# Depthwise-separable convolution: where the last third of the weights is scaled, and how the program ends

## Chip, cores and metric

The kernel runs on one core of a Trainium2 chip. The metric is the device time of one execution in microseconds (us). A run's "span" is the profiled execution, which is some 1.7 to 1.8 us shorter than the time taken for the same run.

Engine names in the profile: PE is TensorE, PEld its weight loads, DVE VectorE, ACT ScalarE, POOL GpSimd, SP the engine that issues the transfers. L162 is line 162 of the kernel concerned.

## The reference

With a depthwise kernel of 1x1 the reference comes down to this, in bf16, with x of 1x384x384x384 and pw of 384x384:

```python
out = x * dw[0, 0]                       # per channel
return einsum('bhwc,cd->bhwd', out, pw)  # 147456 rows x 384 x 384
```

## The kernel before

The channel factors dw are multiplied into pw once, so that x goes straight into the matmuls. The 147456 rows are worked in 288 "supertiles" of 512 rows. For each, VectorE transposes x in blocks of 32x32, and TensorE runs 48 matmuls on quarters of its array (32 rows of contraction each, four side by side; the 48 take 1.951 us). The four quarters hold partitions 0 to 31, 32 to 63 and so on ("quadrants"), and each reads its own copy of the scaled weights `w_r`: 6 blocks of 2 x 384 columns on all 128 partitions. ScalarE copies the results out of PSUM.

The weights are made at the start. pw comes in one transfer; a selection matrix, scaled with dw, spreads its rows to all quadrants by matmul; the results are copied to `w_r`:

```python
nc.sync.dma_start(pw_n[:], pw.rearrange("(k p) d -> p k d", p=P)).then_inc(s_pw, 16)
# (cut: then all loads of x and stores, in order of need)
w_eng = [1, 0, 1, 1, 1, 1]              # who copies block b: 1 ScalarE, 0 VectorE
# (cut)
nc.tensor.wait_ge(s_pw, 16)
for b in range(NB):                     # NB = 6
    # (cut: waits)
    for r in range(2):
        mm = nc.tensor.matmul(w_ps(b)[:, r, :],
            lhsT=sel_w[:, b // 2, 2 * (b % 2) + r, :], rhs=pw_n[:, b // 2, :], start=True, stop=True)
    mm.then_inc(s_w)
for b in (0, 2, 3):
    nc.tensor.wait_ge(*w_done[b])
```

The loop of TensorE leaves out the last four supertiles. Three of those are written out one by one, and the last is worked in two parts of 256 and 128 columns, so that its first part can be copied while the second is computed:

```python
with nc.tensor.Fori(0, NS // 2 - 2, 1) as it:        # NS = 288, two supertiles a round
    rv = nc.tensor.to_reg(it + 1)
    for s in range(2):
        supertile(s, rv)
supertile(0, NS // 2 - 1)
supertile(1, NS // 2 - 1)
supertile(0, NS // 2)
for ps, c0, c1 in ((1, 0, DS), (0, DS, D)):          # DS = 256: the split of the last
    # (cut: 48 matmuls of c1 - c0 columns)
```

Only the last store writes rows of 4 x 384 elements that lie together (3072 bytes); those before it write 768 bytes for each supertile that they hold.

## Time and profile before

| | before |
|---|---|
| time, median of the first 3 runs | 577.61 us (577.1 to 577.85) |
| profiled span | 575.3 us |
| TensorE busy | 567.2 us, 99% of the span |
| VectorE, ScalarE busy | 509.9 and 418.2 us |
| loop of matmuls starts | 7.67 us |
| last copy out of PSUM ends | 569.98 us, 562.31 after the loop's start |
| last store issued, landed | 570.1, 574.0 us |

The middle is bound by TensorE (1.951 us a supertile). So the table is to be read from its lower half: what comes ahead of the loop, and what follows the last matmul, is all that the change can move. The lines that carry this are in the prediction.

### The profile page before, as it was taken

How to read it: one execution, taken by the hardware profiler on the slowest of the kernel's cores; microseconds unless marked ns; L12 is line 12 of the kernel's file. 1: busy time of each engine (PE TensorE's matmuls, PEld its weight loads, DVE VectorE, ACT ScalarE, POOL GpSimd, SP SyncE). 2: the span in 40 equal slices, each digit the busy share in tenths (PEclk: the TensorE clock that was granted, in tenths of full speed). 3: DMA queues.
4: the chain of work that ended last, by engine and by line, in shares of the span. 5: the costliest groups of instructions: out<-in, count | busy, mean ns of one | idle time of the engine just before them, and what ended most of it. 6: DMA issues, size and time to landing. Idle time of an engine off the chain costs nothing.

```text
span 575.3 us, 29802 instructions
## 1 busy us (share of the span) xinstructions
PE 567.2 (99%) x13919; PEld 415.8 (72%) x13919; DVE 509.9 (89%) x584; ACT 418.2 (73%) x297; POOL 1.7 (0%) x8
## 2 busy tenths in 40 slices
PE   8999999999999999999999999999999999999995
PEld 5777777777777777777777777777777777777774
DVE  6999999999999999999999999999999999999994
ACT  6777777777777777777777777777777777777774
POOL 1000000000000000000000000000000000000000
PEclk9999999999999999999999999999999999999999
DMA  8999999999999999999999999999999999998876
GB/s 344 429 399 428 425 415 428 428 430 409 376 411 419 374 399 430 397 390 389 432 398 389 397 429 388 389 401 432 387 394 410 423 390 391 409 402 320 369 282 227
DMA packets 25938, 226.92 MB, mean 394 GB/s; under 512 B 1221, under 2 KB 5702, under 8 KB 22086
## 3 DMA queue, kind: packets, MB, share of 16 engines
q1 hardware_dynamic: 25924, 226.79, 98.0%
q8 instruction: 3, 0.05, 0.0%
q14 instruction: 9, 0.07, 0.0%
q10 hardware_dynamic: 2, 0.00, 0.0%
HBM read 113.54 MB, written 113.25 MB: 394 GB/s over the span
## 4 chain that ended last, share of the span: by engine, by line
PE 98%; ACT 0%; DVE 0%; issue 0%; POOL 0%; POOLq 0%; SPq 0%
PE ps L162 97%; PE ps L181 0%; ACT w_r L292 0%; PE ps L241 0%; DVE O L322 0%; PE ps L212 0%; POOL zero L253 0%; POOL warm L252 0%; POOLq L355 0%; PE ps L196 0%; SPq L99 0%
## 5 line engine op out<-in xcount | busy, mean ns | idle before, releaser
L162 PE MATMUL ps<-w_r,T 32*128 32x384 bf16 x13776 | 559.8, 321 | 0.9 <-ACT w_r L292 0.9
L279 DVE STREAM_TRANSPOSE T<-X 128x384 uint32<-128x384 uint32 x576 | 505.9, 879 | 54.4
L325 ACT CAST O<-ps 128x1536 bf16<-128x1536 f32 x289 | 413.0, 1429 | 148.3 <-PE ps L162 147.7
L162 PEld LDWEIGHTS ps<-w_r,T 32*128 32x128 bf16 x13776 | 411.6, 93 | 149.1 <-issue 1.2
L292 ACT CAST w_r<-ps 128x768 bf16<-128x768 f32 x5 | 3.6, 820 | 1.9 <-PE ps L212 1.9
L181 PE MATMUL ps<-zero 32*128 32x384 bf16 x32 | 2.8, 517 | 1.4 <-POOL zero L253 1.4
L322 DVE CAST O<-ps 128x768 bf16<-128x768 f32 (+2 forms) x3 | 2.1, 691 | 1.4 <-PE ps L162 1.1
L297 DVE COPY dw_f<-ps 128x3 f32<-128x3 f32 x1 | 0.2, 160 | 3.0 <-PE ps L196 3.0
L212 PE MATMUL ps<-pw_n,sel_w 128*128 128x384 bf16 x12 | 2.7, 357 | 0.0
L181 PEld LDWEIGHTS ps<-zero 32*128 32x128 bf16 x32 | 1.1, 118 | 2.0 <-issue 1.7
L212 PEld LDWEIGHTS ps<-pw_n,sel_w 128*128 128x128 bf16 x12 | 1.0, 105 | 1.9 <-issue 0.7
L265 ACT ACT_TABLE_LOAD x1 | 1.3, 1283 | 1.5 <-SPq L99 1.5
L241 PE MATMUL ps<-w_r,T 32*128 32x256 bf16 (+1 forms) x96 | 2.2, 241 | 0.0
L241 PEld LDWEIGHTS ps<-w_r,T 32*128 32x128 bf16 x96 | 2.0, 93 | 0.2
L292 DVE CAST w_r<-ps 128x768 bf16<-128x768 f32 x1 | 1.0, 956 | 1.2 <-PE ps L212 1.2
L301 DVE TENSOR_SCALAR sel_w<-sel,dw_f 128x512 bf16<-128x512 bf16 x3 | 0.9, 347 | 0.1
L255 POOL TENSOR_SCALAR_AFFINE_SELECT sel<-ones 128x512 bf16<-128x512 bf16 x1 | 0.7, 735 | 0.1
L196 PEld LDWEIGHTS ps<-ones,dw_row 1*128 1x128 bf16 x3 | 0.3, 127 | 0.3 <-issue 0.2
L254 POOL MEMSET ones<- 128x512 bf16 x1 | 0.5, 528 | 0.0
L265 ACT COPY warm<-warm 128x1 f32<-128x1 f32 x2 | 0.3, 189 | 0.0
L253 POOL MEMSET zero<- 128x192 uint32 x1 | 0.3, 258 | 0.0
L196 PE MATMUL ps<-ones,dw_row 1*128 1x1 bf16 x3 | 0.3, 174 | 0.0
(5 smaller groups left out, 0.5 us busy)
## 6 DMA issues: line engine op xcount, KB each, us to landing
X<-in_x_dram SPq DMA_DIRECT2D x26, 3840.0 KB, 21.8
out_dram<-O SPq DMA_DIRECT2D x26, 3840.0 KB, 27.8
X<-in_x_dram SPq DMA_DIRECT2D x2, 1536.0 KB, 17.5
out_dram<-O SPq DMA_DIRECT2D x2, 1536.0 KB, 14.6
X<-in_x_dram SPq DMA_DIRECT2D x3, 768.0 KB, 7.5
out_dram<-O SPq DMA_DIRECT2D x3, 768.0 KB, 9.6
X<-in_x_dram SPq DMA_DIRECT2D x1, 2304.0 KB, 19.9
out_dram<-O SPq DMA_DIRECT2D x1, 2304.0 KB, 12.8
```

Of the source, the lines that this page charges most:

```text
L162: mm = nc.tensor.matmul(PS[s][:, q, :D], lhsT=Ts[s][32 * q : 32 * q + 32, b, par::2], rhs=w_r[32 * q : 32 * q + 32, b, par, :], start=(b = ...
L181: nc.tensor.matmul(PS[0][:, i % 4, :D], lhsT=zero[32 * (i % 4) : 32 * (i % 4) + 32, 0:P], rhs=zero[32 * (i % 4) : 32 * (i % 4) + 32, :], s ...
L196: mm = nc.tensor.matmul(PS[1][:, k, D : D + 1], lhsT=dw_row[:, P * k : P * k + P], rhs=ones[0:1, 0, 0:1], start=True, stop=True,)
L212: mm = nc.tensor.matmul(w_ps(b)[:, r, :], lhsT=sel_w[:, b // 2, 2 * (b % 2) + r, :], rhs=pw_n[:, b // 2, :], start=True, stop=True,)
L241: mm = nc.tensor.matmul(PS[ps][:, q, : c1 - c0], lhsT=Ts[1][32 * q : 32 * q + 32, b, par::2], rhs=w_r[32 * q : 32 * q + 32, b, par, c0:c1] ...
L255: nc.gpsimd.affine_select(out=sel[:].rearrange("p (v r) (q w) -> p v r q w", v=2, q=4), in_=ones[:].rearrange("p (v r) (q w) -> p v r q w" ...
L265: c = nc.scalar.copy(warm[:, s + 1 : s + 2], warm[:, 0:1])
L279: ins = nc.vector.transpose(out=Tw[:, 3 * h : 3 * h + 3], in_=Xw[:, :, j, 96 * h : 96 * h + 96].rearrange("p k (b w) -> p b k w", w=32),)
L292: i = nc.vector.tensor_copy(out, in_) if e == 0 else nc.scalar.copy(out, in_)
L301: nc.vector.tensor_scalar_mul(sel_w[:, k], sel[:], dw_f[:, k : k + 1]).then_inc(s_sw)
L322: e = nc.vector.tensor_copy(Ov[:, nq:4, j, c0:c1], PS[ps][:, nq:4, : c1 - c0])
L325: a = nc.scalar.copy(Ov[:, 0:nq, j, c0:c1], PS[ps][:, 0:nq, : c1 - c0])
```

## The change

Its intent: let the loop start earlier by making fewer weights ahead of it, and make the end shorter. It does four things.

1. Only two thirds of pw go through TensorE. The last third is loaded to each quadrant by a transfer of its own (four of 96 KB, 32 partitions each, issued after the first load of x), and GpSimd multiplies it by dw with four instructions of 128x384.
2. The loop waits at its entry for blocks 0 and 1 only. Blocks 2 to 5 are waited for within the first supertile.
3. The loop covers all 288 supertiles: no written-out end, no split.
4. The last three stores (and loads) use the layout with 3072-byte runs of output.

The diff, cut to its core:

```diff
-    pw_n = consts.tile([P, 3, D], BF16, name="pw_n")
+    pw_n = consts.tile([P, 2, D], BF16, name="pw_n")
+    pw_q = consts.tile([P, 2, 2, D], BF16, name="pw_q")
...
-            if t + 1 < NT:
-                dst = of[512 * first : 512 * (first + L), :].rearrange("(q p j) d -> p q (j d)", q=4, p=P)
+            if first + LONG < NS:                       # LONG = 3
+                dst = rows.rearrange("(q p j) d -> p q (j d)", q=4, p=P)
...
-        nc.sync.dma_start(pw_n[:], pw.rearrange("(k p) d -> p k d", p=P)).then_inc(s_pw, 16)
+        for k in range(2):
+            nc.sync.dma_start(pw_n[:, k, :], pw[P * k : P * k + P, :]).then_inc(s_pw[k], 16)
+        load_x(0)
+        pw_v = pw[2 * P :, :].rearrange("(b w r) d -> w b (r d)", w=32, r=2)
+        for q in range(4):
+            dst = pw_q[32 * q : 32 * q + 32].rearrange("w b r d -> w b (r d)")
+            nc.sync.dma_start(dst, pw_v).then_inc(s_pq, 16)
...
-        w_eng = [1, 0, 1, 1, 1, 1]
+        pieces = [(0, 0, 2, 1), (1, 0, 1, 0), (1, 1, 1, 1), (2, 0, 2, 1), (3, 0, 2, 1)]
+        pieces += [(b, r, 1, 2) for b in (4, 5) for r in range(2)]   # block, row, rows, engine (2: GpSimd)
...
+                        if s == 0 and par == 0 and q == 0 and b > 1:
+                            w_ready(b)
...
-        for b in (0, 2, 3):
-            nc.tensor.wait_ge(*w_done[b])
-        with nc.tensor.Fori(0, NS // 2 - 2, 1) as it:
+        for b in range(2):
+            w_ready(b)
+        with nc.tensor.Fori(0, NS // 2, 1) as it:
             rv = nc.tensor.to_reg(it + 1)
             for s in range(2):
                 supertile(s, rv)
-        supertile(0, NS // 2 - 1)
-        supertile(1, NS // 2 - 1)
-        supertile(0, NS // 2)
-        (the split last supertile)
...
+            if e == 2:
+                i = nc.gpsimd.tensor_scalar_mul(out, pw_q[:, b - 4, r : r + n, :], dw_q[:, ...])
+                i._wait_ge(s_pq, 64)
```

`dw_q`, dw laid out for the quadrants, comes from four small matmuls. The last supertile's results are now copied half by ScalarE and half by VectorE, in one go.

More of the change, by code (lines that the diff above doesn't have):

```diff
@@ L14 @@
 NR = 3
-DS = 256
+LONG = 3
 def _groups(n_super: int):
@@ L65 @@
     psum = ctx.enter_context(tc.tile_pool(name="psum", bufs=1, space=bass.MemoryType.PSUM))
-    pw_n = consts.tile([P, 3, D], BF16, name="pw_n")
+    pw_n = consts.tile([P, 2, D], BF16, name="pw_n")
+    pw_q = consts.tile([P, 2, 2, D], BF16, name="pw_q")
     ones = consts.tile([P, 4, P], BF16, name="ones")
     sel = consts.tile([P, 4, P], BF16, name="sel")
-    sel_w = consts.tile([P, 3, 4, P], BF16, name="sel_w")
+    sel_w = consts.tile([P, 2, 4, P], BF16, name="sel_w")
     w_r = consts.tile([P, NB, 2, D], BF16, name="w_r")
     dw_row = consts.tile([1, C], BF16, name="dw_row")
+    dw_b = consts.tile([P, 1], BF16, name="dw_b")
+    dw_q = consts.tile([P, 4], F32, name="dw_q")
     dw_f = consts.tile([P, 3], F32, name="dw_f")
@@ L88 @@
     s_dw = nc.alloc_semaphore("s_dw")
-    s_pw = nc.alloc_semaphore("s_pw")
+    s_pw = [nc.alloc_semaphore(f"s_pw{k}") for k in range(2)]
+    s_pq = nc.alloc_semaphore("s_pq")
     s_df = nc.alloc_semaphore("s_df")
@@ L92 @@
     s_dwf = nc.alloc_semaphore("s_dwf")
+    s_dq = nc.alloc_semaphore("s_dq")
+    s_dwq = nc.alloc_semaphore("s_dwq")
     s_sel = nc.alloc_semaphore("s_sel")
     s_w = nc.alloc_semaphore("s_w")
-    s_wr = [nc.alloc_semaphore(f"s_wr{e}") for e in range(2)]
+    s_wr = [nc.alloc_semaphore(f"s_wr{e}") for e in range(3)]
     s_seed = nc.alloc_semaphore("s_seed")
@@ L102, in load_x @@
             dst = Xs[g % NR][:, 4 * off : 4 * (off + L), :]
-            if t + 1 < NT:
-                src = xf[512 * first : 512 * (first + L), :].rearrange("(p s) c -> p (s c)", p=P)
+            rows = xf[512 * first : 512 * (first + L), :]
+            if first + LONG < NS:
+                src = rows.rearrange("(p s) c -> p (s c)", p=P)
                 dst = dst.rearrange("p s c -> p (s c)")
             else:
-                src = xf[512 * first :, :].rearrange("(a k q) c -> q a k c", k=4, q=4)
+                src = rows.rearrange("(a k q) c -> q a k c", k=4, q=4)
             if i == 0 and g >= NR:
@@ L116, in store @@
             src = Os[g % NR][:, 4 * off * D : 4 * (off + L) * D]
-            if t + 1 < NT:
-                dst = of[512 * first : 512 * (first + L), :].rearrange("(q p j) d -> p q (j d)", q=4, p=P)
+            rows = of[512 * first : 512 * (first + L), :]
+            if first + LONG < NS:
+                dst = rows.rearrange("(q p j) d -> p q (j d)", q=4, p=P)
                 src = src.rearrange("p (q e) -> p q e", q=4)
-                nc.sync.wait_ge(s_a[je % 2], je // 2 + 2)
-                if je >= NS - 2:
-                    nc.sync.wait_ge(s_d, 1)
-            else:
-                dst = of[512 * first :, :].rearrange("(m q) d -> m (q d)", q=4)
-                nc.sync.wait_ge(s_a[1], NS // 2 + 2)
-                nc.sync.wait_ge(s_d, 3)
+            else:
+                dst = rows.rearrange("(m q) d -> m (q d)", q=4)
+            nc.sync.wait_ge(s_a[je % 2], je // 2 + 2)
+            if je + 1 == NS:
+                nc.sync.wait_ge(s_d, 1)
             nc.sync.dma_start(dst, src).then_inc(s_o[g % NR], 16)
         nc.scalar.dma_start(dw_row[:], dw.rearrange("a e c -> a (e c)")).then_inc(s_dw, 16)
-        nc.sync.dma_start(pw_n[:], pw.rearrange("(k p) d -> p k d", p=P)).then_inc(s_pw, 16)
+        for k in range(2):
[5 more added lines that the diff above has]
+            nc.sync.dma_start(dst, pw_v).then_inc(s_pq, 16)
         todo = []
         for t, (g, i, off, first, L) in enumerate(chunks):
-            todo.append((g_end[g - NR] if g >= NR else -1, load_x, t))
+            if t > 0:
+                todo.append((g_end[g - NR] if g >= NR else -1, load_x, t))
             todo.append((first + L + 1, store, t))
@@ L140, with w_ready @@
             nc.sync.wait_ge(s_o[o], 16 * sum(map(len, groups[o::NR])))
-        w_eng = [1, 0, 1, 1, 1, 1]
-        w_done, made = [], [0, 0]
-        for e in w_eng:
+        pieces = [(0, 0, 2, 1), (1, 0, 1, 0), (1, 1, 1, 1), (2, 0, 2, 1), (3, 0, 2, 1)]
+        pieces += [(b, r, 1, 2) for b in (4, 5) for r in range(2)]
+        made = [0, 0, 0]
+        w_done = [[] for b in range(NB)]
+        for b, r, n, e in pieces:
             made[e] += 1
-            w_done.append((s_wr[e], made[e]))
+            w_done[b].append((s_wr[e], made[e]))
         def w_ps(b):
-            return PS[0 if b in (2, 3) else 1][:, 2 * (b % 2) : 2 * (b % 2) + 2, :D]
+            return PS[b // 2][:, 2 * (b % 2) : 2 * (b % 2) + 2, :D]
+        def w_ready(b):
+            for sem, v in w_done[b]:
+                nc.tensor.wait_ge(sem, v)
         def supertile(s, rv):
@@ L171, in supertile @@
                             mm._wait_ge(s_a[s], rv)
-                        elif s == 0 and q == 0 and par == 0:
-                            mm._wait_ge(*w_done[b])
                         if b in (2, 5) and par == 1 and q == 3:
@@ L196 @@
             mm = nc.tensor.matmul(
-                PS[1][:, k, D : D + 1],
+                PS[1][:, 0, D + k : D + k + 1],
                 lhsT=dw_row[:, P * k : P * k + P],
@@ L203 @@
         mm.then_inc(s_df)
-        idle_work(2)
-        nc.tensor.wait_ge(s_pw, 16)
-        for b in range(NB):
+        idle_work(1)
+        nc.tensor.wait_ge(s_sel, 1)
+        nc.tensor.wait_ge(s_dwf, 2)
+        for i in range(4):
+            mm = nc.tensor.matmul(
+                PS[1][:, 3, D + i : D + i + 1],
+                lhsT=sel[:, i, :],
+                rhs=dw_b[:],
+                start=True,
+                stop=True,
+            )
+        mm.then_inc(s_dq)
+        idle_work(1)
+        for b in range(4):
             if b % 2 == 0:
+                nc.tensor.wait_ge(s_pw[b // 2], 16)
                 nc.tensor.wait_ge(s_sw, b // 2 + 1)
-            if b >= 4:
-                nc.tensor.wait_ge(*w_done[b - 4])
+            if b == 2:
+                nc.tensor.wait_ge(s_dwq, 1)
             for r in range(2):
@@ L225 @@
                 supertile(s, rv)
-        supertile(0, NS // 2 - 1)
-        supertile(1, NS // 2 - 1)
-        supertile(0, NS // 2)
-        for ps, c0, c1 in ((1, 0, DS), (0, DS, D)):
-            for b in range(NB):
-                for par in range(2):
-                    for q in range(4):
-                        if par == 0 and q == 0:
-                            if ps == 1 and b in (0, 3):
-                                nc.tensor.wait_ge(s_t[1][b // 3], NS // 2)
-                            if b == 0:
-                                nc.tensor.wait_ge(s_a[ps], NS // 2 + (ps == 0))
-                                if ps == 0:
-                                    nc.tensor.wait_ge(s_d, 1)
-                        mm = nc.tensor.matmul(
-                            PS[ps][:, q, : c1 - c0],
-                            lhsT=Ts[1][32 * q : 32 * q + 32, b, par::2],
-                            rhs=w_r[32 * q : 32 * q + 32, b, par, c0:c1],
-                            start=(b == 0 and par == 0),
-                            stop=(b == NB - 1 and par == 1),
-                            tile_position=(32 * q, 0),
-                        )
-            mm.then_inc(s_pe)
         nc.gpsimd.memset(warm[:], 0.0).then_inc(s_seed)
@@ L287, with w_out @@
         order = [(t, j) for t in range(NT) for j in range(chunks[t][4])]
-        def w_out(b):
-            e = w_eng[b]
-            out, in_ = w_r[:, b, :, :], w_ps(b)
-            i = nc.vector.tensor_copy(out, in_) if e == 0 else nc.scalar.copy(out, in_)
-            i._wait_ge(s_w, b + 1)
+        def w_out(b, r, n, e):
+            out = w_r[:, b, r : r + n, :]
+            if e == 2:
+                i = nc.gpsimd.tensor_scalar_mul(out, pw_q[:, b - 4, r : r + n, :], dw_q[:, 2 * b + r - 8 : 2 * b + r - 7])
+                i._wait_ge(s_pq, 64)
+            else:
+                in_ = w_ps(b)[:, r : r + n, :]
+                i = nc.vector.tensor_copy(out, in_) if e == 0 else nc.scalar.copy(out, in_)
+                i._wait_ge(s_w, b + 1)
             i.then_inc(s_wr[e])
         nc.vector.wait_ge(s_df, 1)
-        nc.vector.tensor_copy(dw_f[:].rearrange("p (k o) -> p k o", o=1), PS[1][:, 0:3, D : D + 1]).then_inc(s_dwf)
+        nc.vector.tensor_copy(dw_f[:], PS[1][:, 0, D : D + 3]).then_inc(s_dwf)
+        nc.vector.tensor_copy(dw_b[:], PS[1][:, 0, D + 2 : D + 3]).then_inc(s_dwf)
         nc.vector.wait_ge(s_sel, 1)
         nc.vector.wait_ge(s_dwf, 1)
-        for k in range(3):
+        for k in range(2):
             nc.vector.tensor_scalar_mul(sel_w[:, k], sel[:], dw_f[:, k : k + 1]).then_inc(s_sw)
-        for b in range(NB):
-            w_out(b)
+        nc.vector.tensor_copy(dw_q[:], PS[1][:, 3, D : D + 4])._wait_ge(s_dq, 1).then_inc(s_dwq)
+        nc.gpsimd.wait_ge(s_dwq, 1)
+        for piece in pieces:
+            w_out(*piece)
         transposes(*order[0])
@@ L312 @@
                 nc.scalar.wait_ge(s_o[g % NR], 16 * sum(map(len, groups[g % NR : g : NR])))
-            if jj + 2 < NS:
-                parts = [(s, 0, D, 4, 2 * jj + 2)]
-            elif jj + 2 == NS:
+            nq = 4
+            if jj + 1 == NS:
+                nq = 2
                 nc.vector.wait_ge(s_o[g % NR], 16 * sum(map(len, groups[g % NR : g : NR])))
-                parts = [(s, 0, D, 2, 2 * jj + 2)]
-            else:
-                parts = [(1, 0, DS, 2, 2 * jj + 1), (0, DS, D, 2, 2 * jj + 2)]
-            for ps, c0, c1, nq, v in parts:
-                if nq < 4:
-                    e = nc.vector.tensor_copy(Ov[:, nq:4, j, c0:c1], PS[ps][:, nq:4, : c1 - c0])
-                    e._wait_ge(s_pe, v)
-                    e.then_inc(s_d)
-                a = nc.scalar.copy(Ov[:, 0:nq, j, c0:c1], PS[ps][:, 0:nq, : c1 - c0])
-                a._wait_ge(s_pe, v)
-                a.then_inc(s_a[s])
+                e = nc.vector.tensor_copy(Ov[:, nq:4, j, :], PS[s][:, nq:4, :D])
+                e._wait_ge(s_pe, 2 * jj + 2)
+                e.then_inc(s_d)
+            a = nc.scalar.copy(Ov[:, 0:nq, j, :], PS[s][:, 0:nq, :D])
+            a._wait_ge(s_pe, 2 * jj + 2)
+            a.then_inc(s_a[s])
             if jj + 2 < NS:
```

## The prediction

> **What bounds the kernel now.** I read the page's groups first, then the chain that ended last in order of time, then the timeline of the first 10 us, then narrow windows at the end. The groups of the page:
>
> ```profile
> L162 PE MATMUL ps<-w_r,T 32*128 32x384 bf16 x13776 | 559.8, 321 | 0.9 <-ACT w_r L292 0.9
> L279 DVE STREAM_TRANSPOSE T<-X 128x384 uint32<-128x384 uint32 x576 | 505.9, 879 | 54.4
> L325 ACT CAST O<-ps 128x1536 bf16<-128x1536 f32 x289 | 413.0, 1429 | 148.3 <-PE ps L162 147.7
> ```
>
> The columns are busy us and mean ns, then the idle before the group. The matmul loop (L162) idles once, 0.9 us, just before its first matmul. From there 287 supertiles of 48 matmuls follow without a hole: 559.83 / 287 = 1.951 us each. DVE and ACT have idle time, so TensorE is the bound for 97% of the span, and the diff leaves that loop's matmuls as they are. Only the two ends are open:
>
> ```profile
> 2.92 1.30 PE ps L181 x11
> 4.22 0.74 PE ps L212 x2
> 4.96 0.02 issue
> 4.98 2.21 ACT w_r L292 x3
> 7.19 0.48 issue
> 7.67 559.83 PE ps L162 x13776
> 567.51 1.33 PE ps L241 x48
> 568.84 0.02 issue
> 568.86 0.69 DVE O L322
> 569.55 0.00 issue
> 569.56 0.42 DVE O L322
> ```
>
> This is the chain, start and length in us. The loop starts at 7.67 because three ACT copies of w_r (2.21 us) end at 7.19, and 0.48 us of sequencer follows. Compute ends at 569.98, yet the span is 575.3. The rest is the last store, issued at 570.1, 3.9 us to landing (574.0), then 1.3 us of closing. The queue's own waits name it, and windows show how few DMA engines work in it (the last two columns are DMA share and GB/s):
>
> ```profile
> SPq L140 <- DMA out_dram<-O: 3.5, 1, 3.5
> 571.00:572.00 1.00, 0.00 (x0) 0.00 (x0) 0.00 (x0) 0.00 (x0) 0.00 (x0) 1.00 0.95 352
> 572.60:573.00 0.40, 0.00 (x0) 0.00 (x0) 0.00 (x0) 0.00 (x0) 0.00 (x0) 1.00 0.11 46
> 573.00:574.10 1.10, 0.00 (x0) 0.00 (x0) 0.00 (x0) 0.00 (x0) 0.00 (x0) 1.00 0.04 17
> ```
>
> 0.11 of 16 engines is about two: most are done by 572.5, and two stragglers hold the end for about 1.5 us. In the packet records one of them is late through the whole tail; the other was held by an instruction fetch of 16 KB (1.34 us) taken about 570.3. The DMA view shows two such fetches after 565:
>
> ```profile
> q8 instruction: 2, 0.03, 1.6%
> ```
>
> The start in the timeline:
>
> ```profile
> 4.14 0.13 PEld L212 LDWEIGHTS ps<-pw_n,sel_w 128*128 128x128 bf16 x2 [0.62 <-DMA pw_n<-in_pw_dram]
> 4.98 3.61 ACT L292 CAST w_r<-ps 128x768 bf16<-128x768 f32 x5 [1.91 <-PE ps L212]
> 5.31 0.96 DVE L292 CAST w_r<-ps 128x768 bf16<-128x768 f32 x1 [1.19 <-PE ps L212]
> 6.18 26.00 DVE L279 STREAM_TRANSPOSE T<-X 128x384 uint32<-128x384 uint32 x28
> ```
>
> The first transposes (0.88 us) end at 7.06, only 0.13 us before the third ACT copy. Behind the weights stands a second limit that nearly coincides.
>
> [...] The new pw loads go to 32 partitions each. No load before is of that shape, so this trace can't say. [...] each loop round already has four separate waits and a branch, and L162 shows no idle from them. [...] The unrolled end is 3 x 96 + 192 = 480 PE instructions[...]; the trace has two 16 KB fetches there. [...] The trace has no GpSimd multiply; its select of 512 elements took 735 ns.
>
> **The change, part by part.**
>
> *Weights.* Two thirds still go through TensorE and copies; ACT drops from five copies of 768 to three and a half. The loop now waits at its entry only for blocks 0 and 1: one copy (0.82), then half of one on ACT (about 0.45, half of 0.82 plus a fixed part), with the other half on DVE, in place of three copies. That is 2.21 - 1.27 = 0.94 us less. But it starts later: TensorE now does 8 idle matmuls, four small ones for dw_q, 8 idle matmuls, then L212. Sixteen idle ones took 1.44 us in the trace; the four small ones add about 0.6 us with load and wait (three took 0.6 us from first load to end). pw's first third lands by about 3.5, earlier than 4.02, but L212 then starts at about 4.8 instead of 4.15: 0.65 lost. Block 0 done 5.3, ACT until 6.1, its half until 6.55, plus 0.48 gives 7.0. DVE ends its half copy at about 6.2 (block 1 at 5.65 plus 0.55) and the first transpose at 7.1, plus 0.2: 7.3. So the loop starts at about **7.3, a gain of 0.4 us**.
>
> *Later weights.* In the loop a block lasts 1.951 / 6 = 0.325 us. Blocks 2 and 3 are ready at 7.35 and 8.15, needed at 7.95 and 8.3. Blocks 4 and 5 come from GpSimd: four pieces at an estimated 0.5 to 0.7 us ([...] the traced select scaled is 0.55) behind the pw_q loads. These are issued at 2.5 to 3.9 (0.45 to 0.49 us an issue)[...]. So block 5 is ready at 8.4 to 9.8 and needed at 8.9: a stall of 0 to 0.9, say **0.2 lost**.
>
> *x loads.* The second x load is issued at about 4.4 instead of 2.0[...]; it and all after it land 0.7 to 1.6 us later (6.6 becomes 7.3 to 8.2; the first long load 24.35 becomes 25.0 to 26.0). TensorE had 1.2 us of slack at supertile 1 and 1.8 later, so most of it is hidden: **0 to 0.3 lost**.
>
> *Loop.* Six waits per round replace five attached ones. Between two existing waits TensorE's sequencer took 48 instructions in at most 0.42 us while the array needs 0.975[...]: **0**. Total matmul time: 288 x 1.951 = 561.8.
>
> *Tail, compute.* The split of the last supertile is removed. Before, compute ended 562.31 us after the loop's start. After: 561.8 + 0.05 + 0.96 (DVE copy of 128x768, as L322 took at 567.55) = 562.8. **0.5 lost.**
>
> *Tail, stores.* Two of the last three stores go from 32 packets of 768 B per engine at 38 ns (1.2 us) to 8 of 3072 B at 121 to 125 ns (0.97): the lagging engine gains 0.25 twice. The final store already had 3072 B. Without the 480 unrolled instructions the fetch at 570.3 should go. The regular lag then ends about 2.4 to 2.9 us after issue instead of 3.9: **1.0 to 1.5 gained**, say 1.3.
>
> Sum: -0.4 + 0.2 + 0.15 + 0.5 - 1.3 = **-0.85 us**. I lean a little further, to -1.2, because the start estimate of L212 is on the cautious side: the small matmuls may run beside the idle ones. 577.6 - 1.2 = **576.4 us**.
>
> **Rivals.** *The narrow loads are the new bound at the start:* if each takes 0.9 us, pw_q lands near 8.5 and the second x load near 9.5. Then block 5 and supertile 1 stall 1.5 to 2 us and the time is 577.5 to 578.5. For it: [...] GpSimd's slow pieces; against it: the DMA has four issues of 0.45 us to spread over. *TensorE pays for the waits inside the loop:* 144 rounds x 0.05 to 0.3 us is 7 to 43 us, 585 to 620. Against it: no idle from the four waits there now. *The store tail is set by fixed latency:* then the last store still lands 3.6 to 3.9 us after issue, like the one at 568.6 (3.6), and the loss of 0.5 us in compute remains: 577.3 to 578. *Everything works:* TensorE's start at 6.6, no stall, store 2.4: 575.
>
> **Range and chances.** No term but the loop rival exceeds 2 us, and 2% is 11.5 us. Low end: start 0.9 earlier, tail 1.5 gained and 0.5 lost, 575.3 with run noise. High end: start stalls eat the gain, the store gains nothing, 577.9. Faster by over 2% needs a change in the loop: 1%. Slower by over 2% is the loop rival: 2%.
>
> **What would show it.** Right: L162 starts near 7.3, holds 561.8 us of 13824 matmuls, with little idle; L241 is gone; the last copy ends about 562.8 after the loop's start; no 16 KB q8 fetch after 565; the last store lands in under 3 us; GpSimd shows four short multiplies ending before 9. Wrong: matmul idle released by GpSimd's w_r or by a transpose that waited for x; a supertile period over 1.951; a last store of 3.6 us or more.

Its sum came to -0.85 us and still has all its terms, but what two of them were worked out with is cut: for the +0.2 of the later weights, the rate at which the new loads land; for the +0.15 of the x loads, the rate of the pw loads ahead of them. No trace had shown either rate (the trace before has no load to 32 partitions, as the text says), so these two terms stand as the forecast's alone, not shown by any number before the run; the first was 3.87 when measured. What remains for the 0 of the loop are the numbers of the trace: 48 instructions in at most 0.42 us against 0.975, and no idle at L162 from the four waits there.

## The result, and the profile after

Ratios here and below are the mean time of one kernel's fast runs over the mean of the other's fast runs of the same rounds, so not quite the ratio of the medians quoted beside them.

| | before | after |
|---|---|---|
| median of 4 runs | 577.49 us | 581.63 us (581.23 to 582.38) |
| ratio | | 1.0073, 95% interval 1.0056 to 1.0091 |
| profiled span | 575.3 us | 579.5 us |

Within 2% the two count as the same, but the change costs 4.1 us where a gain of 1.2 was predicted, and 581.6 us lies above the predicted 575.3 to 577.9.

First the groups of the kernel after, with the same columns as in the prediction (busy us, mean ns, idle before and what ended it):

```profile
L184 PE MATMUL ps<-w_r,T 32*128 32x384 bf16 x13824 | 563.8, 322 | 3.7 <-POOL w_r L300 3.5
L300 POOL TENSOR_SCALAR w_r<-pw_q,dw_q 128x384 bf16<-128x384 bf16 x4 | 4.9, 1246 | 5.3 <-DMA pw_q<-in_pw_dram 5.3
```

Two things are new. The matmuls idle 3.7 us, of which 3.5 were ended by GpSimd's weights. And they are busy 563.8 us where 288 x 1.951 = 561.8 was expected: another 2 us, not idle. The chain that ended last, in order of time (start, length), says where the idle time comes from:

```profile
3.81 3.98 DMA pw_q<-in_pw_dram
7.79 0.09 issue
7.88 4.92 POOL w_r L300 x4
12.80 0.14 issue
12.93 561.86 PE ps L184 x13784
...
574.82 0.96 DVE O L332
```

In the kernel before, this chain ran through ScalarE's copies. Here it runs through the last transfer of `pw_q`, which lands at 7.79, and the four GpSimd multiplications, 4.92 us in all, which end at 12.80. Only then do the last 8 matmuls of the first supertile start (13824 - 13784 = 40 lie before). The timeline shows the loop starting and stopping twice:

```profile
7.43 1.48 PE L184 MATMUL ps<-w_r,T 32*128 32x384 bf16 x32 [0.23 <-DVE T L287]
10.49 0.51 PE L184 MATMUL ps<-w_r,T 32*128 32x384 bf16 x8 [1.58 <-POOL w_r L300]
12.93 1.32 PE L184 MATMUL ps<-w_r,T 32*128 32x384 bf16 x28 [1.93 <-POOL w_r L300]
```

So the loop did start early, at 7.43. Without the stops, matmul 41 would run at 7.43 + 40/48 x 1.951 = 9.06. It runs at 12.93: 3.87 us lost.

The other 2 us are in the windows after the pauses. The columns are busy time of PE, PEld, DVE, ACT and POOL, with the number of instructions, then the granted TensorE clock, the DMA share and GB/s:

```profile
14.00:15.00 1.00, 1.00 (x24) 0.68 (x19) 0.86 (x2) 0.93 (x1) 0.00 (x0) 0.62 1.41 602
15.00:16.00 1.00, 1.00 (x20) 0.64 (x15) 0.37 (x1) 0.00 (x0) 0.00 (x0) 0.50 0.73 313
17.00:18.00 1.00, 1.00 (x23) 0.64 (x16) 0.30 (x1) 0.86 (x1) 0.00 (x0) 0.68 1.13 477
```

Between 14.2 and 17.6 us TensorE was granted half its clock. In the trace's record of the clock this stretch (some expectations call it a window) lasts 3413 ns, so it costs about 1.7 us: the 13784 matmuls took 561.86 us here, and 560.18 in runs that kept the full clock (`mul_act`, shown below, and `wide`). The profiled run of the kernel before kept it from 4.79 us on, to past its last matmul.

The clock bears on the start too. No trace has a clock record for its first microseconds, and there the matmuls go at half rate: in before, matmuls of 384 columns start 320 ns apart until about 4.8 us, and 162 ns apart from then on. In after, the record begins at 7.41, and all eight matmuls that make the weights lie ahead of it, 320 ns apart. The instant differs from run to run: 4.18 to 7.38 us in the nine traces with the old head (the start of the program up to the loop), 5.04 to 7.64 in the ten with the new one. So 7.43 against 7.67 does not compare like with like. Where the full clock came by 5.2 us, the loop started at 7.38 to 7.82 with the old head (six traces) and at 7.07 with the new one (`mul_act`). Where it came at 6.2 us or later, the loop started at 8.28 to 8.30 with the old head (three) and mostly at 7.42 to 7.43 with the new one. By these few traces the new head starts the loop 0.3 to 0.9 us sooner.

At the end, the queue's wait for the last store fell from 3.5 to 1.9 us, and the 16 KB instruction fetches on queue q8 from three in the whole run to one:

```profile
SPq L153 <- DMA out_dram<-O: 1.9, 1, 1.9
q8 instruction: 1, 0.02, 0.0%
```

The last store lands 2.3 us after its issue (575.9), where it took 3.9. All terms together, from the two profiled spans:

| term | us |
|---|---|
| span before | 575.3 |
| loop starts at 7.43 instead of 7.67 (clock at the start not alike, see above) | -0.24 |
| pauses in the first supertile | +3.87 |
| half clock for one stretch | +1.68 |
| last copy ends later after the last block (no split: 562.79 against 562.31) | +0.47 |
| last store lands 2.3 instead of 3.9 us after issue | -1.6 |
| sum (span after: 579.5) | 579.5 |

In the 500 us between, the matmul count of each 100 us is that of the kernel before (2468 to 2472): the waits inside the loop cost nothing.

### The profile page after: what moved, and what is told of

It is laid out like the page before. It is cut to its first block, busy times and chain, and to the rows that moved or that the text cites. A ratio compares the mean times of both kernels' runs of the same rounds, so it can differ in the third digit from the quotient of the medians.

```text
span 579.5 us, 30007 instructions
## 1 busy us (share of the span) xinstructions
PE 569.6 (98%) x13871; PEld 418.7 (72%) x13871; DVE 507.1 (88%) x583; ACT 418.2 (72%) x295; POOL 6.6 (1%) x12
## 4 chain that ended last, share of the span: by engine, by line
PE 97%; POOL 1%; DMA 1%; SPq 0%; DVE 0%; issue 0%
PE ps L184 97%; POOL w_r L300 1%; DMA pw_q<-in_pw_dram 1%; SPq L143 0%; DVE O L332 0%; SPq L138 0%; SPq L118 0%; SPq L365 0%; SPq L105 0%
## 5 line engine op out<-in xcount | busy, mean ns | idle before, releaser
L184 PE MATMUL ps<-w_r,T 32*128 32x384 bf16 x13824 | 563.8, 322 | 3.7 <-POOL w_r L300 3.5
L300 POOL TENSOR_SCALAR w_r<-pw_q,dw_q 128x384 bf16<-128x384 bf16 x4 | 4.9, 1246 | 5.3 <-DMA pw_q<-in_pw_dram 5.3
L304 ACT CAST w_r<-ps 128x768 bf16<-128x768 f32 (+1 forms) x4 | 2.7, 722 | 2.4 <-PE ps L244 2.3
```

The lines of the kernel that those rows point to most:

```text
L184: mm = nc.tensor.matmul(PS[s][:, q, :D], lhsT=Ts[s][32 * q : 32 * q + 32, b, par::2], rhs=w_r[32 * q : 32 * q + 32, b, par, :], start=(b = ...
L300: i = nc.gpsimd.tensor_scalar_mul(out, pw_q[:, b - 4, r : r + n, :], dw_q[:, 2 * b + r - 8 : 2 * b + r - 7])
L304: i = nc.vector.tensor_copy(out, in_) if e == 0 else nc.scalar.copy(out, in_)
```

## The experiments

Seventeen runs of sixteen kernels were made (one kernel twice), in five calls, each call beside runs of the kernel before on the same chip. The medians of the kernel before were 577.15, 577.19, 577.27, 577.62 and 577.34 us. My theory: GpSimd's slow multiplications, behind late transfers, cost the time at the head; the end gains. The rivals, some formed as results came: the half clock costs it on its own; the transfers to 32 partitions are what is slow; the four issues are; at the end, the 3072-byte runs make the gain, or the shorter program does.

### Head and end apart

`tail_only`: the head of before with changes 3 and 4. `head_only`: the head of after (changes 1 and 2) with the end of before. `runs_only`: before with change 4 alone. `loop_only`: before with change 3 alone, that is `tail_only` with `LONG = 1`.

```diff
 # runs_only (of before), its core
-            if t + 1 < NT:
+            if first + LONG < NS:             # LONG = 3
 # loop_only (of tail_only)
-LONG = 3
+LONG = 1
```

> The start of the kernel before (weights all through TensorE) with the whole new end (loop over all supertiles, no split, last three stores in 3072-byte runs). Theory: the loss of the change sits in its start and the end is a net gain of 1.1 us (last store lands 1.6 us sooner after its issue, compute ends 0.5 us later), so about 576.4 us against 577.5, loop start at 7.7, last store landing in about 2.3 us, granted clock 1.00. Rival, the separate waits in the loop cost time: then nothing of that kind is here, as the waits are attached as before, and the same 576.4 results; head_only tells that one. Rival, the late engines in the tail of the profile of before were chance: then 577.5 + 0.5 = 578.0.

> The start of the changed kernel with the end of the kernel before. Theory: late scaled weights cost 3.6 us and the clock window that follows the pauses 1.7 us, so about 577.5 + 5.3 = 582.8 us, TensorE idle of about 3.5 us before the first supertile is through, released by GpSimd's w_r, clock 0.992 to 0.995, and after about 20 us a supertile period of 1.951 us. Rival, the separate waits slow every round: then the period is 1.956 or more in stretches far from the start (40 to 540 us).

> The kernel before, with only the loads and stores of the last three chunks changed to the new layout (stores of 3072-byte runs); unrolled end and split stay. If short packets made the lag of the late engines: last store lands about 2.5 us after issue, 576.1 us. If the instruction fetch did: the 16 KB fetches are still there, the last store lands in 3.4 us or more, 577.1 us.

> The kernel before, with only the loop over all supertiles and without the split; the stores keep their 768-byte runs except the last, as before. If the fetch made the lag: no 16 KB fetch after 560 us, last store in about 2.5 us, 577.5 + 0.5 - 1.4 = 576.6 us. If the short packets did: last store in 3.5 us or more, 577.7 us or more.

| | median us | ratio to before (95%) | last store, issue to landing |
|---|---|---|---|
| tail_only | 576.51 | 0.999 (0.9976 to 1.0004) | 2.7 us |
| head_only | 582.83 | 1.0096 (1.0081 to 1.0112) | 4.2 us |
| runs_only | 577.51 | 1.0012 (0.9998 to 1.0026) | 4.1 us |
| loop_only | 575.95 | 0.9983 (0.997 to 0.9997) | 2.3 us |

The head is what costs: +5.7 us by itself, with the last weights even a little later (last block at 13.37 us; `pw_q` landed at 8.22). The end by itself gains 0.6 us, which is not clear of the noise (its interval reaches above 1). The two do not quite add up: 5.7 - 0.6 = 5.1 us against 4.1 for both together. In the profiles 0.44 of that is the later last block of `head_only` (13.37 against 12.93); the rest was not traced.

What the end gains comes from the loop, not from the runs: `loop_only` is faster than before, just clear of the noise, `runs_only` is not, and `tail_only`, with both, is no faster than `loop_only`. The last store's record, for `runs_only` first (time of the instruction, then time from it to the landing):

```profile
L132 SPq DMA_DIRECT2D out_dram<-O x1: 332/332/332, 570.2 to 570.2; - x1
DMA to landing us min/median/max: 4.1/4.1/4.1
```

and for `loop_only`:

```profile
L127 SPq DMA_DIRECT2D out_dram<-O x1: 344/344/344, 570.3 to 570.3; - x1
DMA to landing us min/median/max: 2.3/2.3/2.3
```

With long runs and the written-out end the store is as late as before; with 768-byte runs and no written-out end it is early. `runs_only` still has its three instruction fetches, one of 16 KB, 1.76 us long, just as the last store is issued.

### What makes the last weights late: GpSimd

`mul_act` does the four multiplications on ScalarE, behind its copies. Only the wait for `dw_q` moves with them.

```diff
-                i = nc.gpsimd.tensor_scalar_mul(out, pw_q[:, b - 4, r : r + n, :], dw_q[:, ...])
+                i = nc.scalar.activation(out, pw_q[:, b - 4, r : r + n, :], COPY, scale=dw_q[:, ...])
```

> The changed kernel with the four scalings of the last third on ScalarE instead of GpSimd; the narrow loads stay as late as they are. Theory, slow GpSimd (1.25 us a piece) is the larger half of the loss: ACT is free of block 3 at 8.1 us, four pieces of about 0.5 us end at 10.1 instead of 12.8, TensorE pauses about 1 us instead of 3.5, the array does not go to half clock: 577.1 us, clock 1.00. Rival, the late loads (landing 7.8 us) alone are to blame: then hardly better than the changed kernel's 581.6, over 580.

Measured 576.96 us, ratio 0.9996 (0.9979 to 1.0012), full clock in all runs. Its group (busy us, mean ns) and the piece of its chain that answers to 7.88 above:

```profile
L300 ACT ACTIVATE w_r<-pw_q,dw_q 128x384 bf16<-128x384 bf16 x4 | 2.2, 633 | 0.0
```

```profile
7.85 2.02 ACT w_r L300 x4
9.88 0.14 issue
10.01 560.18 PE ps L184 x13784
```

The same work takes 2.02 us in place of 4.92. The loop starts at 7.07 (the full clock came at 5.04 in this run), the pauses shrink to 10.01 - 7.07 - 1.63 = 1.31 us, and the half clock is gone. This one line gives back all that the change had lost. It gains nothing on the kernel before, though. The last weights are still too late for the loop, now for two reasons at once: their transfers land at 7.71, and ScalarE's own copies, which come first, end at 7.86.

`pool_half` cuts each GpSimd multiplication into two of 192 columns, to tell a fixed cost from a cost per element.

```diff
-                i = nc.gpsimd.tensor_scalar_mul(out, ...)
+                for c in (0, D // 2):
+                    i = nc.gpsimd.tensor_scalar_mul(out[:, :, c : c + D // 2], ...)
```

> The changed kernel with each GpSimd scaling cut into two of 192 elements. If the 1.25 us are mostly a fixed cost per instruction: eight of about 1.1 us, the last ends near 16.7 us. If they go by elements: eight of about 0.63 us, the last ends near 12.8 us as before.

One run, 583.38 us, state unknown. The group:

```profile
L304 POOL TENSOR_SCALAR w_r<-pw_q,dw_q 128x192 bf16<-128x192 bf16 x8 | 5.9, 761 | 5.1 <-DMA pw_q<-in_pw_dram 5.1
```

Eight of 761 ns against four of 1246: 192 more columns cost 485 ns, so 2.5 ns each, and 0.28 us is fixed. Most of the time is in the elements. My estimate of 0.5 to 0.7 us for 384 was short by half for that reason, not because of a start-up cost.

### What makes the last weights late: the transfers

`early` issues the four transfers of `pw_q` from ScalarE's queue at the start, so that they need not wait behind SP's issues. `early_act` adds the edit of `mul_act` to it.

```diff
-            nc.sync.dma_start(dst, pw_v).then_inc(s_pq, 16)
+            nc.scalar.dma_start(dst, pw_v).then_inc(s_pq, 16)
```

> The changed kernel with the four narrow loads issued from ScalarE's queue right after dw, so that they overlap the issues of SyncE; GpSimd still scales. Theory: they land at about 6 us instead of 7.8, GpSimd's four pieces end at about 11 instead of 12.8, the pause of TensorE shrinks by 1.9 us: 579.7 us if the clock still drops for one window, 578.0 if not. Rival, the late loads alone are to blame: 577 or less.

> Both: early loads and scaling on ScalarE. Theory: ScalarE does its copies until 8.1 us and then the four pieces, so the early landing brings nothing over mul_act: 577.1 us. If the loads are the larger part of mul_act's remaining pause, it is faster than mul_act by up to 1 us.

Both missed. `early`: 583.3 us, 1.0111 (1.0094 to 1.0128), slower than after. `early_act`: 578.77, 1.0035 (1.0018 to 1.0052). The line of the chain of `early` that answers to 3.81 above:

```profile
2.83 6.03 DMA pw_q<-in_pw_dram
```

The last transfer is issued a microsecond sooner and lands at 8.86, a microsecond later; the four take 2.2, 4.0, 5.0 and 6.0 us (in `early_act` the last lands at 9.19). SP, freed of four issues, now sends its loads of x sooner: the second at 2.39 instead of 4.28, the third at 2.86 instead of 4.75, before and just after the last part of `pw_q`. So here the issue from a second engine (2.83 against 3.81) did not bring the landing forward (8.86 against 7.79). That the loads of x in between are the reason is my reading; no run holds them back.

`wide` (a wrong result) loads the same bytes to all 128 partitions in each of the four transfers. `one_issue` (also wrong) loads them with a single transfer of 3072 bytes a partition.

```diff
 # wide
-            nc.sync.dma_start(dst, pw_v).then_inc(s_pq, 16)
+            nc.sync.dma_start(pw_q[:, q // 2, q % 2, :], pw[2 * P :, :]).then_inc(s_pq, 16)
 # one_issue, in place of the four
+        nc.sync.dma_start(pw_q[:].rearrange("p b r d -> p (b r d)"),
+            xf[0:512, :].rearrange("(p s) c -> p (s c)", p=P)).then_inc(s_pq, 16)
```

> WRONG RESULT ON PURPOSE: the four loads of pw_q as 128 partitions x 768 B each instead of 32 partitions x 3072 B, same bytes, same number of issues, same place in the queue; GpSimd still scales. Theory, the few partitions make them slow: they land at about 6.5 us instead of 7.8 and the kernel takes 580.3 us. Rival, the order in the queue and the start of the DMA make them late: landing within 0.4 us of 7.8 and 581.6 us.

> WRONG RESULT ON PURPOSE: pw_q is filled by one load of 128 partitions x 3072 B (the same 384 KB, other data) in place of four loads; GpSimd still scales. If the four issues of 0.47 us each and their separate latencies make the data late: it lands at about 6.0 us instead of 7.8, the second x load lands 1.4 us sooner, and the kernel takes about 579.8 us with the half clock, 578 without. If the bytes ahead in the queue do: it lands at 7.0 us or later.

The transfer in the chain of `wide`, then in that of `one_issue`:

```profile
3.82 3.84 DMA pw_q<-in_pw_dram
```

```profile
2.38 4.18 DMA pw_q<-in_x_dram
```

With 128 partitions the last one lands at 7.66 instead of 7.79. So the number of partitions is not what made the last one late, and GpSimd waits for all four. It is not without effect, though: the first three take 2.9 to 3.0 us each from issue to landing, where they take 3.3 to 3.6 with 32 partitions in after and in the other runs that issue them in this place (`head_only`, `mul_act`, `share`, `pool_half`, `kept_warm`); only the last does not follow (3.84 against 3.8 to 4.4). With one issue all lands at 6.56, between the two expectations: 1.2 us sooner, about what three more issues of 0.43 us take, though this run also differs in the number of partitions and in the source. Even then it takes 4.18 us from issue to landing, for 384 KB; a 96 KB part of pw with little beside it took 1.9 to 2.0. How much of this is the load of x (also 384 KB, issued at 1.91) that is under way beside it, I did not separate: what limits the transfers in the first 7 us stays open.

The times of both (580.25 us, 1.0062; 579.85 us, 1.0045) scatter more than others, and the single runs show why: `wide` took 579.37 and 579.48 us at a mean granted clock of 1.0, and 581.01 and 581.99 at 0.995 and 0.992. `one_issue` ran from 578.11 us (0.998) to 581.64 (0.992). So the same kernel pays for the half clock in some runs and not in others. (A mean of 0.997 to 0.999 need not mean a loss: in the traces the clock also drops after the last matmul (at 574.8 us in before, at 577.4 in after), where it costs nothing.)

### The half clock by itself

`kept_warm` puts 96 idle matmuls ahead of the loop of after, so that TensorE has work until the last weights come. The weights are as late as in after.

```diff
         for b in range(2):
             w_ready(b)
+        idle_work(12)
```

> The changed kernel with 96 idle matmuls (12 rounds of 8) between the first weights and the loop, so that TensorE is busy where it paused before; they end near 11 us, so block 5 still comes at 12.8 us and sets the start as before. Theory, the half clock of 3.4 us at about 14 us is a consequence of the pauses: clock 1.00 (0.998 or more) in every run and 581.6 - 2 = 579.5 us, like the runs of the kernel wide that kept their clock. Rival, the half clock comes from something else at the start: 581 or more, clock 0.992 to 0.995 in some runs.

Measured 579.77 us (579.76 to 579.82 in five runs, clock 0.999 in all), ratio 1.0045 (1.0031 to 1.0059). From its chain:

```profile
6.82 4.68 PE ps L202 x96
...
11.54 561.81 PE ps L185 x13824
```

The loop starts at 11.54 and runs through in 561.81 us: no pause, no half clock. That is even 0.24 us later than the loop of after with its pauses counted as a late start (12.93 - 1.63 = 11.30), and yet the ratio is 0.0028 lower, 1.6 us. The two ratios' intervals just overlap. What carries the point is the clock, 0.999 in all five runs against 0.995 or less in all four of after, and the matmuls' time, 561.8 us in the trace against 563.8 busy. So the pauses' second cost, 1.7 us, is shown apart from the first. Why the cost appears in some runs alone is not shown: pauses of 1.6 and 1.9 us, with 8 matmuls between, came before the drop in after, and after nearly the same ones (1.45 and 1.93) in the profiled run of `wide` there was no drop.

### A division of work that fits: `share`

`share` gives ScalarE three of the four multiplications and GpSimd the last.

```diff
-        pieces += [(b, r, 1, 2) for b in (4, 5) for r in range(2)]
+        pieces += [(4, 0, 1, 3), (4, 1, 1, 3), (5, 0, 1, 3), (5, 1, 1, 2)]   # 3: scaled on ScalarE
```

> The changed kernel with three of the four scalings on ScalarE and one on GpSimd, side by side. Theory: GpSimd's piece ends at 9.1 us, ScalarE's third at 9.4 instead of 9.9 with four (mul_act), so the start gains 0.5 us on mul_act: 576.5 us, clock 1.00. Rival, the late loads now set the start alone: no gain over mul_act, 577.0 us.

Measured 576.40 us, ratio 0.9978 (0.9964 to 0.9991). Now another limit follows close behind. The chain of its profile, of the slowest of its five runs, starts with a load of x, the third:

```profile
4.74 6.87 DMA X<-in_x_dram
...
12.71 557.91 PE ps L185 x13728
```

13824 - 13728 = 96 matmuls, two supertiles, lie ahead of that pause. The `pw_q` transfers had pushed back this load too (issued at 4.74, landed at 11.60). Counted back from there, the loop as good as starts at 12.71 - 96 x 1.951 / 48 = 8.81, no sooner than the old head's 7.38 to 8.30. So the new head gains nothing in this profile, and I take the gain of `share` over before for that of its end; no run has this head with the old end.

### What at the end makes the gain

The end loses three things at once: 480 instructions, the split, and a late instruction fetch. `short_unroll` writes out only the last two supertiles, with the split. `unroll_nosplit` writes out four, without the split; `unroll2` two, without. `late_fetch` is `unroll2` with 48 idle matmuls behind the last real one, to draw a fetch into the last store. `loop_again` repeats `loop_only`. (The expectation of `short_unroll` speaks of 288 pairs less. Its edit takes out 96 pairs, 192 instructions; 288 instructions is what stays written out.)

```diff
 # short_unroll (of before)
-        with nc.tensor.Fori(0, NS // 2 - 2, 1) as it:
+        with nc.tensor.Fori(0, NS // 2 - 1, 1) as it:
-        supertile(0, NS // 2 - 1)
-        supertile(1, NS // 2 - 1)
 # unroll_nosplit (of loop_only); unroll2: NS // 2 - 1, and only the last k
-        with nc.tensor.Fori(0, NS // 2, 1) as it:
+        with nc.tensor.Fori(0, NS // 2 - 2, 1) as it:
+        for k in (NS // 2 - 1, NS // 2):
+            supertile(0, k)
+            supertile(1, k)
 # late_fetch (of unroll2)
+        nc.tensor.wait_ge(s_a[0], NS // 2 + 1)
+        for i in range(48):
+            nc.tensor.matmul(PS[0][:, i % 4, :D], lhsT=zero[...], rhs=zero[...], ...)
```

> The kernel before with only the last two supertiles outside the loop (288 unrolled matmul pairs of instructions less: 2 supertiles moved into the loop), split and stores as before. If the late 16 KB fetch at 570 us holds the last store, and the shorter unrolled end does without it: last store lands in 2.3 to 2.7 us, 577.2 - 1.5 = 575.7 us. If a fetch still comes within 3 us of the last store: no change, 577.2 us.

> loop_only once more, on the chip of short_unroll, to see whether its gain over the kernel before (1.2 us, ratio 0.9983) repeats: 0.998, last store in 2.3 us.

> The kernel before with four supertiles unrolled after the loop and no split of the last one; stores as before. It has the unrolled end (384 matmuls and weight loads beyond the loop) but the compute end and the spacing of stores of loop_only. Theory, the instruction fetch holds the last store: one or two 16 KB fetches after 560 us, last store lands in 3.5 us or more, 577.2 + 0.5 = 577.7 us. Rival, the split (and the stores only 1.5 us apart that it makes) does: last store in 2.3 to 2.7 us and 576.0 us, as loop_only.

> The kernel before with two supertiles unrolled after the loop, no split, stores as before: control for late_fetch. Theory: no 16 KB fetch after 567 us, last store lands in 2.3 to 2.8 us, ratio 0.998.

> unroll2 with 48 idle matmuls behind the last supertile in TensorE's program, which nothing waits for and which end before the last store would: only the program is longer, as long as that of short_unroll. Theory, a 16 KB fetch near the last store holds it: one comes after 568 us and the last store lands in 3.3 us or more, 1 us slower than unroll2. Rival, the split held it: last store in 2.3 to 2.8 us, time as unroll2. If no fetch comes after 567 us the run tells nothing.

| | median us | ratio to before (95%) | split | 16 KB fetch near the last store | last store |
|---|---|---|---|---|---|
| before | 577.49 | | yes | 1.34 us | 3.9 us |
| runs_only | 577.51 | 1.0012 (0.9998 to 1.0026) | yes | 1.76 us | 4.1 us |
| head_only | 582.83 | 1.0096 (1.0081 to 1.0112) | yes | 1.75 us | 4.2 us |
| short_unroll | 577.13 | 0.9997 (0.9984 to 1.001) | yes | 0.97 us | 3.5 us |
| unroll2 | 577.02 | 0.9994 (0.9981 to 1.0008) | no | 1.05 us | 2.8 us |
| late_fetch | 576.98 | 0.9994 (0.9981 to 1.0008) | no | 1.37 us | 3.0 us |
| unroll_nosplit | 576.53 | 0.9982 (0.9969 to 0.9996) | no | none (one at 566.1) | 2.3 us |
| loop_only, loop_again | 575.95, 576.08 | 0.9983 in both | no | none | 2.3 us |

In `short_unroll` a fetch still came, and the time stayed, as its second expectation has it. `unroll2` missed: I had expected no fetch so late. It served all the better. Among these kernels without the split, the last store lands after 2.8 and 3.0 us with a 16 KB fetch beside it, and after 2.3 without, whether the end is written out (`unroll_nosplit`) or not. So writing the end out is harmless as such, and where the fetch falls seems to matter, by 0.5 to 0.7 us. That is one profile each, and the ratios' intervals overlap (0.9981 to 1.0008 against 0.997 to 0.9997 of `loop_only`): likely, not shown. `late_fetch` lies between its two expectations.

One value warns: `tail_only` has no late 16 KB fetch and no split, and its last store took 2.7 us. Its trace has an 8 KB instruction fetch (queue q14, 0.31 us) begun 0.27 us before that store; `loop_only` and `unroll_nosplit` have one 0.9 us before theirs, `unroll2` and `late_fetch` 0.6. Whether that is the cause was not tested.

With the split the store comes 1.2 to 1.9 us later than 2.3, and by and large the later the longer the fetch. There the last three stores are issued within 3.0 us (567.07 to 570.08 in before) instead of 3.5 (`loop_only`), which may add to it. A kernel with the split and without a late fetch was not among the runs, so the split's own share stays open.

`loop_only` beats both kernels, twice with an interval below 1: 0.17%, about one microsecond (`unroll_nosplit`, 0.18%, and `share`, 0.22%, do too). In the profiles, kernels with the old head start their loops between 7.38 and 8.30 us, with nothing changed there but the instant at which the full clock comes, so a gain of this size can be read from repeated times only, not from one span.

## Why the prediction was wrong, by its own steps

- **Weights, start of the loop:** 7.3 predicted, 7.43 measured, and the first transpose is what the loop waited for, as predicted. Right, but with some luck in the number: the weights' matmuls ran at half rate in this run, which the estimate does not have; with the full clock early the same head started at 7.07 (`mul_act`).
- **Later weights: the step that failed.** "A stall of 0 to 0.9, say 0.2 lost" was 3.87. Two terms in it were mis-sized, both the same way. The four GpSimd pieces were put at 0.5 to 0.7 us each, and took 1.246 (4.92 for four). The transfers landed at 7.79, later than I had put it from a rate that no trace had shown. So block 5 was ready at 12.8 instead of 8.4 to 9.8. The larger part is GpSimd's: its work alone on ScalarE takes 2.9 us out (`mul_act`). I had scaled the estimate from an affine select (735 ns for 512 elements), which is a different operation; the trace had no GpSimd multiplication to measure, and I took a substitute for evidence.
- **A term that is missing:** the clock. A pause of TensorE was counted at its length. Here it cost 1.7 us more (`kept_warm`); the mean granted clock was 0.992 or 0.995 in all four runs of after, and 1.0 in the profiled run of before (0.997 to 1.0 in its runs of the later calls; in all nine traces with the old head the only drop comes after the last matmul).
- **x loads:** the second load landed at 9.4, later than the 7.3 to 8.2 given. It did not show in after, because the weights were later still; in `share` the third load became the limit.
- **Loop:** 0, measured 0. Right, and the rival of 7 to 43 us is out.
- **Tail, compute:** +0.5, measured +0.47. Right.
- **Tail, stores:** -1.3, measured -1.6; the reason was half wrong. The long runs, counted at 0.25 us twice, brought nothing (`runs_only`). The fetch that it named (its record begins at 569.86, not 570.3) is gone, and so is the split, which it did not count here; how the gain divides between them stays open.
- **The rivals:** the one about narrow loads saw the right place, the head, and the wrong cause (`wide` clears it). It put the loss at 1.5 to 2 us. None of the four had GpSimd's duration as the bound, although the text named "GpSimd's slow pieces" as speaking for the first.

The sum was to be -0.85, leaning to -1.2. With 3.87 in place of 0.2, 1.68 added, and the rest about as predicted, it is +4.2.

## What to carry to other kernels

Before work moves to an engine that the trace has not shown at that operation, measure one instruction of it at its real shape: here one would have given 1.25 us against ScalarE's 0.63, and shown the stall beforehand. A pause of TensorE near the start can cost more than its length, in some runs only, because the clock may drop for a stretch after it (3.4 us here, 6.8 in `pool_half`); look at the granted clock whenever a matmul group's busy time grows. And when the end of a program is trimmed, look whether an instruction fetch falls beside the last store (2.8 and 3.0 us to its landing with one of 16 KB here, 2.3 without, one profile each), before crediting the shape of the transfers.
